# Attention scores on quarter tiles of TensorE, in one pipeline over all batches

## The chip, the cores and the metric

The kernel runs on one core of a Trainium2 chip. The metric is the device time of one launch in microseconds (us); the median of three runs of the kernel before is 711.85 us (710.91 to 712.35). A profile of one further execution shows what each engine did: TensorE (PE; PEld is its loading of weights), VectorE (DVE), ScalarE (ACT), GpSimd (POOL) and SyncE (SP, which issues the transfers).

## What is computed

A causal attention with a window of 64 keys, and an RWKV channel mix on its output. Eight batches, eight heads, 576 positions, head size 64; the model has 512 channels, the mix 1024.

```python
def _attn_ref(q, k, v):                       # (8, 8, 576, 64)
    scores = scale * np.matmul(q, k.transpose(0, 1, 3, 2))
    rel = pos[:, None] - pos[None, :]
    scores = np.where((rel >= 0) & (rel < 64), scores, -1e9)
    ...                                       # softmax over keys
    return np.matmul(attn, v)
def _moe_ref(x, mu_k, mu_r, w_k, w_v, w_r):   # x: (8, 576, 512)
    xk = mu_k * x + (1.0 - mu_k) * x_prev     # x_prev: one position back
    xr = mu_r * x + (1.0 - mu_r) * x_prev
    k = np.maximum(xk @ w_k, 0.0)
    return 1.0 / (1.0 + np.exp(-(xr @ w_r))) * (k * k @ w_v)
```

## The kernel before

**Attention.** A pair of heads fills the 128 partitions: rows 0 to 63 of `q` and `k` belong to one head, 64 to 127 to the other. The 576 queries are nine blocks of 64; a block sees its own keys and those of the block before, 128 in all. One product on the full array makes the scores of a block for both heads (L149). For that the queries stand in `qbd` with zeros where one head's rows meet the other head's columns: `qbd` is 128 rows by (block, head, 64), so the stationary operand is 128x128 of which half is zero. Three blocks are a group (`G`), three groups a pair, and the 32 pairs (8 batches, 4 pairs each) have 288 blocks.

A group runs through these steps, with the tile names that the profile shows:

- `s`, scores on PE (L149, PSUM pool `ps_s`, two buffers), float32; the profile has two instructions for each float32 product.
- `sm` and `nmax` on DVE (L152): mask, scale, minimum; `pr` and `sums` on ACT (L155): the exponential; `rs` on DVE (L158, L159); `pr` times `rs` on POOL (L161).
- `t`, the transposes of the three weights on PE (L168), copied to `pt` by ACT (L170).
- `x`, weights times values on PE (L182): the heads' outputs go to the two halves of the partitions, so each product uses half of the array's columns. Two groups go together (12 products), and ACT copies the result to `xT` (L187).

**Channel mix.** A unit is half a batch, 288 positions; there are 16 units. `time_mix` (L221 to L226) makes `xr` and `xk` on DVE, ACT and POOL. Then come 4 products with `w_r`, 8 with `w_k` and 4 with `w_v`, each 128 outputs wide and accumulated over 12, 12 and 24 instructions (`m`, L235, float32r, PSUM pool `ps_m`, four buffers). ACT, POOL and DVE work on the results (`e`, `th`, `r`; `kf`, `ks`; `r` again), and the output leaves by SP. A unit has 240 instructions of `m`, the kernel 3840.

**Weights.** They come as float64 in 20 chunks of 512 KB (`wst`, L102); five DVE instructions for each chunk (L107 to L113) make float32 of it, ACT and POOL split it in two float32r parts (L116, L117). `w_r` has 4 chunks, `w_k` 8, `w_v` 8, in that order. The first product with `w_v` needs the last chunks.

**Order.** `attention` is a generator of steps for one batch (42 steps); `batches` chains them. At the start 42 steps run, with a chunk of weights at every third from the sixth on; then the first unit's mixing, then `LEAD` = 8 steps more. After that each of a unit's 20 steps takes one or, every 16th time, two attention steps. What the code writes is a priority: a scheduler of the framework orders each engine's instructions, so the order on an engine is not the order of the code.

Of the kernel before, what the change touches and what calls it, by code (L numbers as in the profile page):

```python
# [9 lines left out]
F32 = mybir.dt.float32  # L10
# [3 lines left out]
ALU = mybir.AluOpType  # L14
# [9 lines left out]
NG = NB // G  # L24
# [6 lines left out]
STAGES = 3 * (NP * NG + 2)   # steps of a batch's attention  # L31
# [11 lines left out]
def attn_rwkv_kernel(ctx, tc, qT, kT, v2, mu_k, mu_r, w_k, w_v, w_r, out):  # L43
# [12 lines left out]
    # queries of a pair by block, the heads' apart: zero where a head's rows meet the  # L56
    # other head's columns
    qbd = [const.tile([P, NB, 2, W], F32, name=f"qbd{i}") for i in range(2)]
    nc.vector.memset(qbd[0][:, :G], 0.0)
    nc.vector.memset(qbd[0][:, G:], 0.0)  # L60
# [7 lines left out]
    mask0 = const.tile([P, W], F32, name="mask0")  # L68
    nc.gpsimd.memset(mask, 0.0)
    nc.gpsimd.memset(mask0, 0.0)  # L70
    for h in range(2):
        m = mask[h * W:(h + 1) * W]
        nc.gpsimd.affine_select(out=m, in_=m, compare_op=ALU.is_ge, fill=NEG, base=-1,
                                pattern=[[1, P]], channel_multiplier=-1)
        nc.gpsimd.affine_select(out=m, in_=m, compare_op=ALU.is_ge, fill=NEG, base=W,
                                pattern=[[-1, P]], channel_multiplier=1)
        m = mask0[h * W:(h + 1) * W]
        nc.gpsimd.affine_select(out=m, in_=m, compare_op=ALU.is_ge, fill=NEG, base=0,
                                pattern=[[-1, W]], channel_multiplier=1)

    nc.gpsimd.memset(qbd[1], 0.0)
    # the first group's weights: its first block has none for the other keys
    pr0 = const.tile([P, G, P], F32, name="pr0")
    nc.gpsimd.memset(pr0[:, 0, W:], 0.0)
# [36 lines left out]
    loaded = {}  # L121

    def load_pair(n, cuts=(0, NB)):
        """cuts: the blocks at which q and k are cut into transfers."""
        q = qbd[n % 2]
        k = ld.tile([P, S], F32, name="k")
        for i0, i1 in zip(cuts, cuts[1:]):
            nc.sync.dma_start(k[:, i0 * W:i1 * W], kT[n, :, i0 * W:i1 * W])
            for h in range(2):
                nc.sync.dma_start(q[h * W:(h + 1) * W, i0:i1, h, :],  # L130
                                  qT[n, h * W:(h + 1) * W, i0 * W:i1 * W].rearrange("p (i r) -> p i r", r=W))
        v = ld.tile([P, 2, 4, P], F32, name="v")
        nc.sync.dma_start(v, v2[n])
        loaded[n] = (q, k, v)

    def scores(n, g):
        q, k, _ = loaded[n]
        ps = ps_s.tile([P, G, P], F32, name="s")
        # sm = -(scaled and masked scores), nmax = their minimum
        sm = at.tile([P, G, P], F32, name="sm", bufs=3)  # L140
        nmax = at.tile([P, G], F32, name="nmax", bufs=4)
        pr = pr0 if g == 0 else at.tile([P, G, P], F32, name="pr")
        sums = at.tile([P, G], F32, name="sums", bufs=4)
        # keys of a block's window: the block before and the own one, if there are two
        nks = [W if g == 0 and j == 0 else P for j in range(G)]
        for j, nk in enumerate(nks):
            i = G * g + j
            k0 = (i + 1) * W - nk
            nc.tensor.matmul(ps[:, j, :nk], q[:, i].rearrange("p h r -> p (h r)"),  # L149
                             k[:, k0:k0 + nk], start=True, stop=True)  # L150
# [216 lines left out]
```

## Time and profile before

| | |
|---|---|
| median of 3 runs | 711.85 us |
| span of the profiled execution | 711.3 us |
| PE busy | 682.2 us (96%), 5856 matmul instructions |
| DVE busy | 415.5 us (58%) |
| ACT busy | 413.9 us (58%) |
| POOL busy | 364.9 us (51%) |
| data moved | 56.61 MB, mean 80 GB/s |

In the page's second part each engine has a line of 40 digits, one for each 17.8 us of the span, with the busy share in tenths. The ends of matmuls are modelled and overlap the next ones; so what an instruction costs PE is read from the starts of the instructions around it and not from its own duration. A timeline row gives start, length, engine, line, operation, `out<-in`, the shape and how many instructions are merged in the row (`x12`).

### The profile page before, as it was taken

Reading aid. Unit: us, or ns where it says so; the run is one execution under the profiler, and the core shown is the slowest. Engines: PE = TensorE matmul, PEld = TensorE weight load, DVE = VectorE, ACT = ScalarE, POOL = GpSimd, SP = SyncE. Lnnn points to the kernel's source line nnn. Section 1 sums busy time; section 2 is a strip of 40 time slices with the busy share of each in tenths; the row PEclk is TensorE's granted clock in tenths of the full one; section 3 lists DMA queues with packets and bytes.
Section 4 is the critical chain, followed back from the end, with each engine's and each line's share of the span. In section 5 each row is a group of like instructions: output and inputs, shape, how many; then the busy total and the mean of one; then the engine's idle time right before and its main releaser. Section 6 shows DMA issues by size and latency. Waiting matters only on the chain.

```text
span 711.3 us, 15989 instructions
## 1 busy us (share of the span) xinstructions
PE 682.2 (96%) x5856; PEld 657.9 (92%) x5856; DVE 415.5 (58%) x1326; ACT 413.9 (58%) x1397; POOL 364.9 (51%) x580
## 2 busy tenths in 40 slices
PE   6878878999999999999999999999999999999998
PEld 5766777799999999999999999999999999999998
DVE  3999999955545455465535455463645556463421
ACT  4768775663626383748566575756756475644351
POOL 4788898754335272554626355453624546252420
PEclk9999898999999999999999999999999999999999
DMA  8885666620000001221222222211323221000000
GB/s 208 237 234 152 189 178 176 166 73 26 10 34 2 34 31 64 65 89 45 85 63 72 68 64 88 73 55 44 95 66 94 67 64 48 18 1 35 26 9 34
DMA packets 59742, 56.61 MB, mean 80 GB/s; under 512 B 40592, under 2 KB 49040, under 8 KB 59664
## 3 DMA queue, kind: packets, MB, share of 16 engines
q1 hardware_dynamic: 59664, 55.59, 26.7%
q8 instruction: 46, 0.75, 0.5%
q14 instruction: 32, 0.26, 0.1%
HBM read 46.14 MB, written 9.44 MB: 78 GB/s over the span
## 4 chain that ended last, share of the span: by engine, by line
PE 80%; DVE 15%; POOL 1%; issue 1%; DMA 1%; SPq 1%; ACT 0%
PE m L235 68%; PE s L149 6%; PE x L182 4%; PE t L168 3%; DVE sm L152 2%; DVE wt L111 2%; DVE wt L107 2%; DVE wt L113 2%; DVE xm L224 1%; DVE wt L109 1%; DVE wt L108 1%; DVE rs L158 1%; POOL pr L161 1%; DMA qbd<-qT 1%; DVE d L221 1%
## 5 line engine op out<-in xcount | busy, mean ns | idle before, releaser
L235 PE MATMUL m<-ks,wv_s 128*128 128x288 f32 x1536 | 226.1, 301 | 1.0 <-ACT wv_s L116 0.9
L235 PE MATMUL m<-xk,wk_s 128*128 128x288 f32 x1536 | 221.2, 299 | 2.0 <-POOL wk_s L117 2.0
L161 POOL TENSOR_SCALAR pr<-pr,rs 128x128 f32<-128x128 f32 (+1 forms) x288 | 129.7, 467 | 173.0 <-DVE rs L159 62.4
L235 PEld LDWEIGHTS m<-ks,wv_s 128*128 128x128 f32 x1536 | 208.7, 190 | 2.5 <-ACT wv_s L116 1.3
L235 PEld LDWEIGHTS m<-xk,wk_s 128*128 128x128 f32 x1536 | 207.0, 189 | 3.6 <-POOL wk_s L117 2.2
L155 ACT ACTIVATE pr<-sm,nmax 128x128 f32<-128x128 f32 (+1 forms) x288 | 111.6, 391 | 68.0 <-DVE nmax L152 67.9
L263 POOL TENSOR_TENSOR kf<-kf 128x288 f32<-128x288 f32 x128 | 93.2, 733 | 81.1 <-ACT kf L262 80.1
L266 DVE TENSOR_TENSOR ks<-kf,ks 128x288 fp32r<-128x288 f32 x128 | 72.6, 571 | 71.5 <-ACT ks L265 71.3
L235 PE MATMUL m<-xr,wr_s 128*128 128x288 f32 x768 | 113.1, 299 | 1.0 <-POOL xr L226 1.0
L235 PEld LDWEIGHTS m<-xr,wr_s 128*128 128x128 f32 x768 | 103.5, 188 | 2.4 <-POOL xr L226 1.9
L149 PE MATMUL s<-k,qbd 128*128 128x128 f32 (+1 forms) x576 | 88.4, 294 | 15.7 <-DVE nmax L152 9.0
L149 PEld LDWEIGHTS s<-k,qbd 128*128 128x128 f32 x576 | 79.0, 205 | 19.0 <-DVE nmax L152 11.2
L226 POOL TENSOR_TENSOR xr<-xm,xr 128x288 fp32r<-128x288 f32 x64 | 56.4, 891 | 71.2 <-ACT xr L225 68.4
L152 DVE CUSTOM_DVE_ANT_0 sm<-s,mask 128x128 f32<-128x128 f32 (+1 forms) x288 | 66.7, 276 | 36.1 <-PE s L149 36.0
L262 ACT ACTIVATE kf<-m 128x288 f32<-128x288 f32 x128 | 52.2, 409 | 36.8 <-PE m L235 29.5
L224 DVE SCALAR_TENSOR_TENSOR xm<-d,muk,xT 128x288 f32<-128x288 f32 x64 | 55.2, 862 | 26.7 <-POOL xr L226 26.6
L265 ACT CAST ks<-kf 128x288 fp32r<-128x288 f32 x128 | 55.1, 431 | 24.9 <-POOL kf L263 24.5
L253 DVE SCALAR_TENSOR_TENSOR r<-th,e 128x288 f32<-128x288 f32 x64 | 34.2, 535 | 50.4 <-ACT th L251 50.1
L247 ACT ACTIVATE e<-m 128x288 f32<-128x288 f32 x64 | 26.2, 410 | 60.9 <-PE m L235 60.7
L168 PE MATMUL t<-ident,pr 128*128 128x128 f32 x288 | 55.4, 284 | 6.2 <-POOL pr L161 3.4
L275 DVE SCALAR_TENSOR_TENSOR r<-m,r 128x288 f32<-128x288 f32 x64 | 28.3, 451 | 56.4 <-PE m L235 56.4
L226 POOL TENSOR_TENSOR xk<-xm,xk 128x288 fp32r<-128x288 f32 x64 | 58.5, 933 | 5.2 <-ACT xk L225 5.2
(44 smaller groups left out, 652.7 us busy)
## 6 DMA issues: line engine op xcount, KB each, us to landing
v<-v SPq DMA_DIRECT2D x32, 512.0 KB, 3.6
outT<-r SPq DMA_DIRECT2D x64, 144.0 KB, 1.7
k<-kT SPq DMA_DIRECT2D x31, 288.0 KB, 3.1
qbd<-qT SPq DMA_DIRECT2D x62, 144.0 KB, 3.6
wst<-w_k SPq DMA_DIRECT2D x8, 512.0 KB, 4.1
wst<-w_v SPq DMA_DIRECT2D x8, 512.0 KB, 3.6
wst<-w_r SPq DMA_DIRECT2D x4, 512.0 KB, 7.6
k<-kT SPq DMA_DIRECT2D x1, 192.0 KB, 2.4
```

What stands on the lines that cost most here:

```text
L149: nc.tensor.matmul(ps[:, j, :nk], q[:, i].rearrange("p h r -> p (h r)"), k[:, k0:k0 + nk], start=True, stop=True)
L152: nc.vector.tensor_tensor_reduce(sm[:, j, :nk], ps[:, j, :nk], mask if nk == P else mask0, scale=-SCALE, scalar=FAR, op0=ALU.add, op1=ALU.min,
L155: nc.scalar.activation(pr[:, j, :nk], sm[:, j, :nk], AF.Exp, bias=nmax[:, j:j + 1], scale=-1.0, accum_out=sums[:, j:j + 1])
L161: nc.gpsimd.tensor_scalar(pr[:, j, :nk], pr[:, j, :nk], rs[:, j:j + 1], 1.0, op0=ALU.mult, op1=ALU.mult)
L168: nc.tensor.transpose(ps[:, j, :], pr[:, j, :], ident)
L224: nc.vector.scalar_tensor_tensor(xm, d, mu[:, c:c + 1], xp, op0=ALU.mult, op1=ALU.add)
L226: nc.gpsimd.tensor_sub(xs[:, 1, c], xm, xs[:, 0, c].bitcast(F32))
L235: nc.tensor.matmul(ps, w[:, a, c, col * P:(col + 1) * P], x(c, e), start=(i == 0), stop=(i == last))
L262: nc.scalar.activation(kf, ps, AF.Relu)
L263: nc.gpsimd.tensor_mul(kf, kf, kf)
L265: nc.scalar.copy(ks[:, 0], kf)
L266: nc.vector.tensor_sub(ks[:, 1], kf, ks[:, 0].bitcast(F32))
```

## The change

- **Scores.** `q` is loaded as it is, without zeros. A product takes the 64 rows of one head and the 64 queries of one block as the stationary operand, and 128 keys: it uses a quarter of the array, the row half by the head and the column half by the block. Four such products cover two blocks of both heads. A round is three tiles of two blocks (`slots`), 12 products; the two heads' scores lie in two PSUM tiles. Score products are 576, not 288. DVE, ACT and POOL have as many instructions for them as before (a tile holds two blocks of one head, not one block of two); the 32 that were 64 keys wide are 128 wide.
- **PSUM.** `ps_s` has four buffers (two before), `ps_m` two (four before).
- **Order.** Two pairs are one item of three rounds. `attention` runs over all batches without a break, in four steps for each round; 32 steps run ahead with a chunk of weights at every second from the fifth on, and afterwards the steps are due at 24 for each 40 steps of the mix. `mix_v` takes one round, 12 products.
- **Buffers.** `q`, `k`, `v` have three buffers; `sm` two and not three, `pr` four, `xm` two.

How the scheduler's order changes PE's work, in the middle of the kernel. Each row is a run of like matmuls (`s` scores, `t` transposes, `x` weights times values, `m` channel mix; the last column is the shape of the moving operand, or of the half that is written, and the number of products). Before, from the products with `w_r` of one unit into those with `w_k`:

```order
L235 MATMUL m<-xr,wr_s 128x288 x12
L168 MATMUL t<-ident,pr 128x128 x3
L235 MATMUL m<-xr,wr_s 128x288 x12
L182 MATMUL x<-pt,v 64x64 x12
L235 MATMUL m<-xr,wr_s 128x288 x12
L149 MATMUL s<-k,qbd_83 128x128 x3
L235 MATMUL m<-xr,wr_s 128x288 x12
L168 MATMUL t<-ident,pr_114 128x128 x3
L235 MATMUL m<-xk,wk_s 128x288 x24
L149 MATMUL s<-k,qbd_83 128x128 x3
```

In that stretch PE leaves the full-width array once, for 12 products `x` in a row. At a like place of the changed kernel:

```order
L144 MATMUL s<-k,q 64x128 x2
L183 MATMUL x<-pt,v 64x64
L144 MATMUL s<-k,q 64x128 x3
L246 MATMUL m<-xk,wk_s 128x288 x12
L144 MATMUL s<-k,q 64x128 x3
L246 MATMUL m<-xk,wk_s 128x288 x12
L170 MATMUL t<-ident,pr 128x128 x3
L183 MATMUL x<-pt,v 64x64 x10
L246 MATMUL m<-xk,wk_s 128x288 x24
L170 MATMUL t<-ident,pr 128x128 x3
L183 MATMUL x<-pt,v 64x64
L144 MATMUL s<-k,q 64x128 x6
```

Here it leaves it four times, and runs of `s` and `x` are cut into pieces of 1 to 10 products. Over the whole kernel PE goes from the full array to a part of it and back 70 times before, and 191 times now; 54 times it now goes directly between `s` and `x`, which use different parts. Of the 191 returns, 151 are to `m` and 40 to `t`.

SP's queue at the start (transfers, in the order of issue). Before:

```order
L128 DMA k<-kT 128x576
L130 DMA qbd_83<-qT 64x9x64 x2
L133 DMA v<-v 128x1024
L102 DMA wst<-w_r 128x1024
L128 DMA k<-kT 128x576
L130 DMA qbd_82<-qT 64x9x64 x2
L102 DMA wst<-w_r 128x1024 x2
```

This stands behind the loads of the first pair and of `mu_k`, `mu_r`: the first weights come behind two pairs. Now, behind the same loads:

```order
L122 DMA k<-kT 128x576
L123 DMA q<-qT 128x576
L125 DMA v<-v 128x1024
L122 DMA k<-kT 128x576
L123 DMA q<-qT 128x576
L125 DMA v<-v 128x1024
L96 DMA wst<-w_r 128x1024 x3
```

The first weights now come behind three pairs, and a pair's queries are one transfer.

The diff, cut to the parts that are spoken of:

```diff
-    ps_s = ctx.enter_context(tc.tile_pool(name="ps_s", bufs=2, space=PSUM))
+    ps_s = ctx.enter_context(tc.tile_pool(name="ps_s", bufs=4, space=PSUM))
...
-    ps_m = ctx.enter_context(tc.tile_pool(name="ps_m", bufs=4, space=PSUM))
+    ps_m = ctx.enter_context(tc.tile_pool(name="ps_m", bufs=2, space=PSUM))
...
     def load_pair(n, cuts=(0, NB)):
-        q = qbd[n % 2]
-        k = ld.tile([P, S], F32, name="k")
+        q = ld.tile([P, S], F32, name="q", bufs=3)
+        k = ld.tile([P, S], F32, name="k", bufs=3)
         for i0, i1 in zip(cuts, cuts[1:]):
             nc.sync.dma_start(k[:, i0 * W:i1 * W], kT[n, :, i0 * W:i1 * W])
-            for h in range(2):
-                nc.sync.dma_start(q[h * W:(h + 1) * W, i0:i1, h, :],
-                                  qT[n, h * W:(h + 1) * W, i0 * W:i1 * W].rearrange("p (i r) -> p i r", r=W))
+            nc.sync.dma_start(q[:, i0 * W:i1 * W], qT[n, :, i0 * W:i1 * W])
...
+    def slots(n, g):
+        if g == 1:
+            return [((n, 6), (n, 7)), ((n, 8), (n + 1, 8)), ((n + 1, 6), (n + 1, 7))]
+        n += g // 2
+        return [((n, i), (n, i + 1)) for i in range(0, 2 * G, 2)]
...
-            nc.tensor.matmul(ps[:, j, :nk], q[:, i].rearrange("p h r -> p (h r)"),
-                             k[:, k0:k0 + nk], start=True, stop=True)
+        for e, halves in enumerate(sl):
+            for j, (n, i) in enumerate(halves):
+                q, k, _ = loaded[n]
+                k0 = max(i - 1, 0) * W
+                for h in range(2):
+                    hr = slice(h * W, (h + 1) * W)
+                    nc.tensor.matmul(ps[h][j * W:(j + 1) * W, e, :], q[hr, i * W:(i + 1) * W],
+                                     k[hr, k0:k0 + P], start=True, stop=True)
+        return [soft(ps[h], sl) for h in range(2)]
...
-    for i in range(STAGES):
+    first = STEPS * (ROUNDS + 2)
+    for i in range(first):
         run(ats, 1)
-        if i >= 5 and i % 3 == 0:
+        if i >= 4 and i % 2 == 0:
             run(wl, 1)
...
-            run(ats, 1)
-            if done % 16 == 0:
-                run(ats, 1)
+            due = (done + LEAD) * ROUNDS * STEPS // MOE_STEPS
+            run(ats, due - ran)
+            ran = due
```

More of the change, by code (lines that the diff above doesn't have):

```diff
@@ L23 @@
 G = 3
-NG = NB // G
+NG = 3
 TH = S // 2
@@ L66, in attn_rwkv_kernel @@
     mask = const.tile([P, P], F32, name="mask")
-    mask0 = const.tile([P, W], F32, name="mask0")
+    mask0 = const.tile([P, P], F32, name="mask0")
     nc.gpsimd.memset(mask, 0.0)
     nc.gpsimd.memset(mask0, 0.0)
-    for h in range(2):
[L72 to L84, printed above, removed]
+    for j in range(2):
+        for t in (mask, mask0):
+            m = t[j * W:(j + 1) * W]
+            if t is mask0 and j == 0:
+                nc.gpsimd.affine_select(out=m, in_=m, compare_op=ALU.is_ge, fill=NEG, base=0,
+                                        pattern=[[-1, P]], channel_multiplier=1)
+                continue
+            nc.gpsimd.affine_select(out=m, in_=m, compare_op=ALU.is_ge, fill=NEG, base=-1,
+                                    pattern=[[1, P]], channel_multiplier=-1)
+            nc.gpsimd.affine_select(out=m, in_=m, compare_op=ALU.is_ge, fill=NEG, base=W,
+                                    pattern=[[-1, P]], channel_multiplier=1)
     muk = const.tile([P, NC], F32, name="muk")
@@ new lines, in scores @@
+    def scores(sl):
+        ps = [ps_s.tile([P, G, P], F32, name="s") for _ in range(2)]
+        for e, halves in enumerate(sl):
[7 more added lines that the diff above has]
+        return [soft(ps[h], sl) for h in range(2)]
@@ L141, in scores, with soft @@
+    def soft(ps, sl):
+        sm = at.tile([P, G, P], F32, name="sm", bufs=2)
         nmax = at.tile([P, G], F32, name="nmax", bufs=4)
-        pr = pr0 if g == 0 else at.tile([P, G, P], F32, name="pr")
+        pr = at.tile([P, G, P], F32, name="pr", bufs=4)
         sums = at.tile([P, G], F32, name="sums", bufs=4)
[L145 to L149, printed above, removed]
-                             k[:, k0:k0 + nk], start=True, stop=True)
@@ L166, in flip @@
         ps = ps_t.tile([P, G, P], F32, name="t")
-        for j in range(G):
-            nc.tensor.transpose(ps[:, j, :], pr[:, j, :], ident)
+        for e in range(G):
+            nc.tensor.transpose(ps[:, e, :], pr[:, e, :], ident)
         pt = at.tile([P, G, P], F32, name="pt", bufs=3)
```

106 lines of the change are left out of this document (53 added, 53 removed).

## Prediction

> **What bounds the kernel now.** The page's slices come first, those of PE and of DVE:
>
> ```profile
> PE   6878878999999999999999999999999999999998
> DVE  3999999955545455465535455463645556463421
> ```
>
> In the first eight slices (142 us) DVE is full and PE is not; from there on it is the other way round. DVE's last decode of a weight, in the timeline, marks the border, and a table of the stages (PE, PEld, DVE, ACT, POOL busy; then clock, DMA share, GB/s) shows both sides:
>
> ```profile
> 140.27 0.74 DVE L113 SCALAR_TENSOR_TENSOR wt<-wst,wt 128x512 uint32<-128x512 uint32 x1
> ...
> 0.00:141.00 141.00, 115.78 (x1029) 99.50 (x1029) 125.85 (x470) 95.90 (x361) 112.37 (x173) 0.94 0.68 191
> 141.00:628.50 487.50, 486.78 (x4227) 478.91 (x4227) 258.26 (x804) 287.64 (x953) 227.95 (x377) 1.00 0.19 57
> ```
>
> Up to 141 us DVE decodes and holds the rest: the products with `w_v` need the last chunks. Most of its 15 idle us lie in the first slice. Behind that PE has no gap, and no other engine is busy for 60% of the time. So the time is 141 us, plus what PE has left then, plus a tail; the tail is 3.1 us, since the chain's last piece ends at 708.19 of 711.3:
>
> ```profile
> 628.57 79.62 PE m L235 x600
> ```
>
> **What an instruction costs PE.** Modelled ends overlap, so I take starts. Four stretches of PE's timeline, and one piece of the chain, give everything:
>
> ```profile
> 404.06 1.84 PE L235 MATMUL m<-xr,wr_s 128*128 128x288 f32 x12
> 405.83 0.92 PE L182 MATMUL x<-pt,v 128*64 128x64 f32 x24
> 406.68 1.85 PE L235 MATMUL m<-xr,wr_s 128*128 128x288 f32 x12
> 408.37 0.83 PE L149 MATMUL s<-k,qbd 128*128 128x128 f32 x6
> 408.95 0.52 PE L235 MATMUL m<-xr,wr_s 128*128 128x288 f32 x2
> ```
>
> ```profile
> 244.49 1.84 PE L235 MATMUL m<-xr,wr_s 128*128 128x288 f32 x12
> 246.26 0.57 PE L182 MATMUL x<-pt,v 128*64 128x64 f32 x12
> 246.76 1.85 PE L235 MATMUL m<-xr,wr_s 128*128 128x288 f32 x12
> ...
> 250.28 5.28 PE L235 MATMUL m<-xk,wk_s 128*128 128x288 f32 x38
> 255.39 0.49 PE L168 MATMUL t<-ident,pr 128*128 128x128 f32 x3
> 255.63 0.65 PE L235 MATMUL m<-xk,wk_s 128*128 128x288 f32 x3
> ```
>
> ```profile
> 330.06 3.18 PE m L235 x24
> ```
>
> - `m`: 24 take 3.18 us, 0.1325 each.
> - `s`: from 406.68 to 408.95 are 2.27 us with 12 `m` (1.59) and 6 `s`: 0.68, so 0.113 for one full-width instruction over 128 keys.
> - `t`: from 250.28 to 255.63 are 5.35 us with 38 `m` (5.04): 0.31 for three, 0.105 each.
> - `x`: with 24 instructions from 404.06 to 406.68 are 2.62 us, less 1.59: 1.03. With 12, from 244.49 to 246.76: 2.27 less 1.59, 0.68. So 0.0292 for an instruction, and **0.33 for the visit**: to leave the full array for half of its columns and come back costs as much as 11 such instructions.
>
> PE's groups from 145.94 us on (counts are what matters here) test these prices:
>
> ```profile
> L235 PE MATMUL m<-ks,wv_s 128*128 128x288 f32 x1440 | 207.8, 299 | 0.0
> L235 PE MATMUL m<-xk,wk_s 128*128 128x288 f32 x1440 | 203.7, 298 | 0.0
> L235 PE MATMUL m<-xr,wr_s 128*128 128x288 f32 x720 | 104.6, 299 | 0.0
> L149 PE MATMUL s<-k,qbd 128*128 128x128 f32 (+1 forms) x306 | 42.9, 275 | 0.0
> L168 PE MATMUL t<-ident,pr 128*128 128x128 f32 x174 | 30.7, 272 | 0.0
> L182 PE MATMUL x<-pt,v 128*64 128x64 f32 x708 | 28.0, 226 | 0.0
> ```
>
> With the order's 34 visits: 3600 x 0.1325 + 306 x 0.113 + 174 x 0.105 + 708 x 0.0292 + 34 x 0.33 = 477.0 + 34.6 + 18.3 + 20.7 + 11.2 = 561.8 us. The trace has 708.19 - 145.94 = 562.3. PE there waits for nothing.
>
> **The first stage of the changed kernel.** Ahead of DVE's last decode stood 123 `sm`, 38 pairs of `rs`, 11 `d`, 19 `xm`, 4 `r` and 8 `ks`; now there stand 72, 22, 7, 12, 4 and 0. Gone are 51 `sm`, 16 pairs, 4 `d`, 7 `xm`, 8 `ks`. An `sm` follows the last after 0.21 us in the timeline, and the groups give the rest:
>
> ```profile
> 141.01 0.28 DVE L152 CUSTOM_DVE_ANT_0 sm<-s,mask 128x128 f32<-128x128 f32 x1
> ...
> 141.22 0.28 DVE L152 CUSTOM_DVE_ANT_0 sm<-s,mask 128x128 f32<-128x128 f32 x1
> ```
>
> ```profile
> L266 DVE TENSOR_TENSOR ks<-kf,ks 128x288 fp32r<-128x288 f32 x128 | 72.6, 571 | 71.5 <-ACT ks L265 71.3
> L224 DVE SCALAR_TENSOR_TENSOR xm<-d,muk,xT 128x288 f32<-128x288 f32 x64 | 55.2, 862 | 26.7 <-POOL xr L226 26.6
> L224 DVE SCALAR_TENSOR_TENSOR xm<-d,mur,xT 128x288 f32<-128x288 f32 x64 | 43.0, 673 | 8.9 <-POOL xk L226 8.6
> L221 DVE TENSOR_TENSOR d<-xT 128x288 f32<-128x288 f32 x64 | 37.4, 591 | 11.4 <-ACT xT L187 10.8
> L158 DVE TENSOR_SCALAR rs<-sums 128x3 f32<-128x3 f32 x96 | 24.0, 250 | 26.9 <-ACT pr L155 26.8
> L159 DVE RECIPROCAL rs<-rs 128x3 f32<-128x3 f32 x96 | 16.2, 169 | 1.5
> ```
>
> 51 x 0.21 + 16 x 0.42 + 4 x 0.59 + 7 x 0.77 + 8 x 0.57 = 10.7 + 6.7 + 2.4 + 5.4 + 4.6 = 30 us less. Against that the first weights stand behind one pair more, 1.06 MB:
>
> ```profile
> GB/s 208 237 234 152 189 178 176 166 73 26 10 34 2 34 31 64 65 89 45 85 63 72 68 64 88 73 55 44 95 66 94 67 64 48 18 1 35 26 9 34
> ...
> v<-v SPq DMA_DIRECT2D x32, 512.0 KB, 3.6
> k<-kT SPq DMA_DIRECT2D x31, 288.0 KB, 3.1
> qbd<-qT SPq DMA_DIRECT2D x62, 144.0 KB, 3.6
> ```
>
> At the 208 GB/s of the first slice that is 5 us; `q` in one piece may take some of it back, so 4 (0 to 5). The masks' 32 wider tiles, the `qbd` zeros and the fewer transfers later lie beside other work: nothing. The stage ends at 141 - 30 + 4 = **115 us** (107 to 120).
>
> This is work moved, not saved: it comes later, where DVE has room, but PE has less behind it. I put PE at 96 `m` by then. DVE's and ACT's orders then have four `r` results and two `kf` behind them, 72 `m`, and two `ps_m` buffers hold 24 more.
>
> **What PE has left there.** By its order from that row on, 3744 `m`, 231 `t`, 936 `x` and 834 `s` instructions, 161 visits and 38 direct changes between `s` and `x`.
>
> - `m` 496.1 and `t` 24.3: old prices.
> - Visits: 161 x 0.33 = 53.1. Before it was 11.2 behind the border; this is the large term. The cover that hid the others was DVE's stage. No row shows a visit to quarter tiles; PE leaves the same full array for it, so I take the same price (0.2 to 0.33 for the about 70 that begin with `s`).
> - Direct changes: no row. Between nothing and a whole visit; half, 0.165, makes 6.3 (0 to 12.5). The Trainium skill (TensorEngine Tiling (Array Packing), Key Properties) says that a change of the tiling mode, though not of the tile, drains TensorE. By that none of the 38 is free; no run here shows one.
> - `x`: 936 x 0.0292 = 27.3. Pieces of odd length leave a half idle: taken run by run from the order, at 2 x 0.0584 for a product alone, 3.9 more. 31.2.
> - `s`: the disputed one. Bounds: 0.113, the full-width row over the same 128 keys, if tiles run one by one, and a quarter of it if four run at once. The nearest row is `x`: 0.0292 for 64 columns is half of 0.113 x 64 / 128, so two tiles do run at once. A table of the first moments of a visit shows how:
>
> ```profile
> 405.82:405.85 0.03, 0.02 (x2) 0.02 (x2) 1.00 0.00 0
> ...
> 405.82:405.94 0.12, 0.11 (x3) 0.11 (x5) 1.00 0.00 0
> ```
>
> A visit (the columns are PE, PEld, clock, DMA share, GB/s): two start together, the third 0.1 us later. A product's two instructions go to the same tile; if the second held up the next product, the first would start alone. I read it as tiles that do not wait for each other, and take 0.0292: 834 x 0.0292 = 24.4, and 9.5 for pieces that don't fill four tiles: 33.9.
>
> Sum: 496.1 + 24.3 + 53.1 + 6.3 + 31.2 + 33.9 = 644.9 us. `ps_m` with two buffers is a new wait: PE's next product but one needs the last result read. Cover is a product of 12 `m`, 1.59 us, against a read of 0.4:
>
> ```profile
> L155 ACT ACTIVATE pr<-sm,nmax 128x128 f32<-128x128 f32 x256 | 100.6, 396 | 34.6 <-DVE nmax L152 34.6
> L262 ACT ACTIVATE kf<-m 128x288 f32<-128x288 f32 x128 | 52.2, 409 | 36.8 <-PE m L235 29.5 <-DVE ks L266 6.5 <-issue 0.2
> ```
>
> Only where three exponentials (1.2 us) stand ahead of the read on ACT is PE, with all that is queued on it, late by a few tenths; once or twice in each of 16 units makes 0 to 10, and I take 4. In all 115 + 644.9 + 4 + 3.1 = **767 us**; by the same account the kernel before has 711.3, 0.5 from the median.
>
> **Rivals.**
>
> - *Two tiles at once.* If matmuls start strictly in order, the second instruction of a product waits for the first, and only its end overlaps the next product: two at a time, 0.0584 each, 48.7 and 10.4 for the pieces, 25 more: **792 us**. For it: two is all that the trace shows. Against it: the two that start together. The Trainium skill (TensorE: Matmul & The Clock Gate, The mechanism) gives it as the rule: matmuls start and end in program order. The two first starts above don't agree with that, as far as the records are true.
> - *No tiles at once in the row halves or at all* (the change does not do what it says): `s` 97.4 us, **831 us**. Against it: `x` has two at once.
> - *Visits are cheap*, the one way to the other side: if leaving for quarter tiles and halves in a mixed order costs nothing, 59.4 us fall away and it is **708 us**, faster through the shorter first stage. It decides from 0.02 us a visit down. Against it: 0.33 in both rows.
>
> **How the numbers follow.** Four at once 0.52, two 0.28, one 0.12, cheap visits 0.04, and 0.04 for a first stage that I misread either way. The time is that of the likeliest, 767; with its bounds (first stage -8 to +5, visits -9, direct changes -6 to +6, waits -4 to +6) it alone would be 745 to 785. Two at once lies within 770 to 810. The range 742 to 812 holds nearly all of both. About 0.2% can be told from no change: faster 0.04, same 0.01, slower 0.95.
>
> **What would show it.** Right: DVE's last decode near 115 us; PE full from there; `s` in runs of 12 products at about 0.7 us beside 0.33 for the visit, against 1.4 if two run at once; a gap of about 0.3 around each piece of `x`. Wrong: PE with idle time behind the border that ACT's reads of `m` end; visits whose price is far from 0.33; or a last decode at 130 us or later.

## The result, and the profile after

| | before | after |
|---|---|---|
| median of four runs, us | 712.1 (710.9 to 712.6) | 765.8 (764.5 to 766.1, and 801.5) |
| ratio | 1 | 1.0754 [1.0738, 1.0769] |
| profiled execution: its time, its span | 711.3 span | 764.5, 762.7 span |
| DVE's last decode ends | 141.0 | 111.7 |
| what PE has behind that | 567 | 648 |

The run of the kernel after at 801.5 us was in a slower state, at a lower granted clock (0.824 against 0.95 to 1.00); without it the median is 765.5 us.

The change made the kernel slower by 53.7 us. The slices of PE, of DVE and of the granted clock in the page of the changed kernel:

```profile
PE   5877889999999999999999999999999999999998
DVE  4998995345463444544345544534446343554522
PEclk9755599999999999999999999999999999999999
```

The picture is the one of before with its border moved ahead: DVE is full for the first six slices instead of eight, and PE from the seventh on. The timeline of DVE gives the border, and the table of the stages both sides (PE, PEld, DVE, ACT, POOL busy, then clock, DMA share and GB/s):

```profile
111.00 0.68 DVE L107 SCALAR_TENSOR_TENSOR wt<-wst,wt 128x512 uint32<-128x512 uint32 x1
```

```profile
0.00:111.70 111.70, 86.67 (x710) 65.92 (x710) 96.67 (x314) 60.94 (x219) 82.87 (x111) 0.71 0.57 196
111.70:759.60 647.90, 645.34 (x5722) 594.77 (x5722) 296.26 (x1010) 354.82 (x1178) 274.55 (x469) 1.00 0.17 53
```

So 29 us were won in the first stage, and 81 lost behind it, where PE is busy for 645.3 of 647.9 us and the granted clock is 1.00, as it was before. The table of waits for PE from 111.7 us on, and the chain's last piece, say that this is not idle time, and that the tail is the old one (759.6 of 762.7):

```profile
PE s L144 <- DVE nmax L155: 2.0, 1, 2.0
PE m L246 <- DVE r L286: 1.3, 4, 0.4
```

```profile
721.19 38.41 PE m L246 x288
```

Where it is lost stands in PE's timeline (start, time, count at the end of the row). Here `s` is a quarter-tile product, which is two instructions:

```profile
149.55 1.85 PE L246 MATMUL m<-xr,wr_s 128*128 128x288 f32 x12
151.32 0.43 PE L144 MATMUL s<-k,q 64*64 64x128 f32 x2
151.68 1.86 PE L246 MATMUL m<-xk,wk_s 128*128 128x288 f32 x12
...
238.47 1.85 PE L246 MATMUL m<-xr,wr_s 128*128 128x288 f32 x12
240.25 0.45 PE L144 MATMUL s<-k,q 64*64 64x128 f32 x8
240.63 1.86 PE L246 MATMUL m<-xk,wk_s 128*128 128x288 f32 x12
...
243.54 1.85 PE L246 MATMUL m<-xk,wk_s 128*128 128x288 f32 x12
245.32 0.34 PE L183 MATMUL x<-pt,v 128*64 128x64 f32 x4
245.58 1.85 PE L246 MATMUL m<-xk,wk_s 128*128 128x288 f32 x12
```

Take starts, less the 1.59 us of 12 `m`. From 238.47 to 240.63 are 2.16: four products of `s` cost 0.57. From 243.54 to 245.58 are 2.04: two products of `x` cost 0.45. From 149.55 to 151.68 are 2.13: one product of `s` alone costs 0.54, nearly as much as four. Counted over the trace behind the last decode, PE leaves the full array 160 times and changes directly between `s` and `x` 36 times; before it left it 34 times.

### The profile page after: what moved, and what is told of

It reads as the page before. It is cut to its first block, busy times and chain, and to the rows that moved or that the text cites. A ratio compares the mean times of both kernels' runs of the same rounds, so it can differ in the third digit from the quotient of the medians.

```text
span 762.7 us, 17032 instructions
## 1 busy us (share of the span) xinstructions
PE 732.0 (96%) x6432; PEld 660.7 (87%) x6432; DVE 393.4 (52%) x1324; ACT 415.8 (55%) x1397; POOL 357.4 (47%) x579
## 2 busy tenths in 40 slices
DMA packets 26578, 56.68 MB, mean 74 GB/s; under 512 B 3200, under 2 KB 11904, under 8 KB 26496
## 4 chain that ended last, share of the span: by engine, by line
PE 80%; DVE 12%; POOL 3%; issue 2%; DMA 1%; ACT 1%; SPq 0%; POOLq 0%
PE m L246 65%; PE x L183 6%; PE s L144 6%; PE t L170 4%; DVE xm L235 2%; DVE sm L155 1%; DVE wt L103 1%; DVE wt L105 1%; POOL pr L164 1%; DVE wt L102 1%; DVE wt L107 1%; DMA wst<-w_r 1%; DVE wt L101 1%; DVE d L232 1%; DVE rs L161 1%
## 5 line engine op out<-in xcount | busy, mean ns | idle before, releaser
L246 PE MATMUL m<-ks,wv_s 128*128 128x288 f32 x1536 | 214.7, 298 | 1.3 <-DVE r L286 1.3
L164 POOL TENSOR_SCALAR pr<-pr,rs 128x128 f32<-128x128 f32 x288 | 130.2, 468 | 139.3 <-DVE rs L162 91.9
L246 PE MATMUL m<-xr,wr_s 128*128 128x288 f32 x768 | 121.7, 309 | 1.7 <-ACT xr L236 1.0
L158 ACT ACTIVATE pr<-sm,nmax 128x128 f32<-128x128 f32 x288 | 112.8, 396 | 16.6 <-DVE nmax L155 16.4
L144 PE MATMUL s<-k,q 64*64 64x128 f32 x1152 | 88.4, 320 | 21.4 <-DVE nmax L155 13.3
L144 PEld LDWEIGHTS s<-k,q 64*64 64x64 f32 x1152 | 55.2, 151 | 40.0 <-DVE nmax L155 16.0
L155 DVE CUSTOM_DVE_ANT_0 sm<-s,mask 128x128 f32<-128x128 f32 x288 | 66.1, 283 | 23.9 <-PE s L144 23.9
L183 PEld LDWEIGHTS x<-pt,v 128*64 128x64 f32 x1152 | 53.3, 150 | 25.3 <-issue 20.8
L183 PE MATMUL x<-pt,v 128*64 128x64 f32 x1152 | 71.7, 246 | 1.7 <-ACT xT L189 1.7
L235 DVE SCALAR_TENSOR_TENSOR xm<-d,mur,xT 128x288 f32<-128x288 f32 x64 | 52.5, 820 | 17.2 <-POOL xr L237 13.9
```

What stands on the lines that cost most here:

```text
L144: nc.tensor.matmul(ps[h][j * W:(j + 1) * W, e, :], q[hr, i * W:(i + 1) * W], k[hr, k0:k0 + P], start=True, stop=True)
L155: nc.vector.tensor_tensor_reduce(sm[:, e], ps[:, e], mask0 if sl[e][0][1] == 0 else mask, scale=-SCALE, scalar=FAR, op0=ALU.add, op1=ALU.m ...
L158: nc.scalar.activation(pr[:, e], sm[:, e], AF.Exp, bias=nmax[:, e:e + 1], scale=-1.0, accum_out=sums[:, e:e + 1])
L164: nc.gpsimd.tensor_scalar(pr[:, e], pr[:, e], rs[:, e:e + 1], 1.0, op0=ALU.mult, op1=ALU.mult)
L183: nc.tensor.matmul(ps[h * W:(h + 1) * W, o, :], v[:, a, c, h * W:(h + 1) * W], pts[h][:, e, j * W:(j + 1) * W], start=True, stop=True)
L235: nc.vector.scalar_tensor_tensor(xm, d, mu[:, c:c + 1], xp, op0=ALU.mult, op1=ALU.add)
```

## The experiments

The theory is that of the prediction: the loss is the price of 160 visits, which come from the order in which the scheduler puts the small pieces, and not from the quarter tiles. The rivals are that the new deal of PSUM's banks (two buffers for `m`) makes PE wait; that quarter-tile products are dear in themselves; and that a visit is cheap. The first four runs hold PE's order, and cut its runs or undo a part of the change; the next four follow from their misses; the last four, and e6, leave the order to the scheduler. The table has them all, with the visits and the direct changes behind the last decode as counted in each trace, the start of the last decode, the time from there to PE's last end, and the median. All but the median are of the one profiled execution; that of e11 took 709.5 us, 3.8 above its median.

| run | visits, direct | last decode | PE behind it | median, us |
|---|---|---|---|---|
| before | 34, 0 | 140.3 | 567.9 | 712.1 |
| after | 160, 36 | 111.0 | 648.6 | 765.8 |
| e1 whole runs, held | 78, 0 | 109.1 | 621.2 | 737.2 |
| e2 and `x` beside `s` | 39, 37 | 115.3 | 610.6 | 732.0 |
| e3 e1 with runs cut | 152, 0 | 117.3 | 636.4 | 758.4 |
| e4 e1 with padded scores, late queries | 39, 0 | 130.3 | 607.2 | 742.8 |
| e5 e1 with 4 `m` buffers | 77, 0 | 112.0 | 609.1 | 724.7 |
| e6 after with 4 `m` buffers | 98, 2 | 133.3 | 585.9 | 726.9 |
| e7 e1 with padded scores | 39, 0 | 129.1 | 607.0 | 742.4 |
| e8 e2 with 4 `m` buffers, held from unit 2 | 36, 33 | 130.0 | 577.3 | 711.5 |
| e9 e2's code, 4 `m` buffers, lead 16, not held | 40, 31 | 130.7 | 568.0 | 703.8 |
| e10 the same, lead 15 | 74, 33 | 129.8 | 583.8 | 718.9 |
| e11 the same, lead 9 | 40, 33 | 130.1 | 574.4 | 705.7 |
| e12 e9 with padded scores | 33, 0 | 137.9 | 568.7 | 711.5 |

### e1: PE's order held, so that runs are whole

```diff
+    def pin(ins):
+        return tc.keep_in_program_order(ins)
-                    nc.tensor.matmul(ps[h][j * W:(j + 1) * W, e, :], ...)
+                    pin(nc.tensor.matmul(ps[h][j * W:(j + 1) * W, e, :], ...))
```

The same stands at the transposes, at `x` and at `m`.

> The changed kernel with one difference: every instruction of TensorE is held in the order of the code, so that the 12 quarter-tile products of a group (s) and its 12 half-tile products (x) each run as one piece. By its order 89 visits to part tiles and 6 direct changes between s and x are left, of 191 and 54; the same instructions, pools and data. Theory (the visits are the loss): behind the last decode 77 visits and no direct change are left, so 496.1 for m, 24.6 for t, 28.1 for x, 24.6 for s and 77 x 0.33 = 25.4, about 599 us after 96 m, 604 after 72; with a first stage of 106 to 112 us that is 708 to 722 us, most likely 714, some 50 below the changed kernel. Rival 1 (two ps_m buffers: the new wait is the loss): the buffers are the same and a fixed order hides a wait worse, so 760 us or more. Rival 2 (quarter-tile products are themselves dear, whatever their order): all 1152 instructions are still there, so 750 us or more.

It took 737.2 us, 1.0367 [1.0349, 1.0384] of before. That is 28.5 below the changed kernel, which neither rival gives, and 15 above the theory's upper end. PE's timeline and its table of waits from 112 us on say why:

```profile
193.74 1.85 PE L250 MATMUL m<-xk,wk_s 128*128 128x288 f32 x12
195.52 0.89 PE L148 MATMUL s<-k,q 64*64 64x128 f32 x24
196.33 3.44 PE L250 MATMUL m<-xk,wk_s 128*128 128x288 f32 x24
...
203.37 1.84 PE L250 MATMUL m<-xk,wk_s 128*128 128x288 f32 x12
205.13 0.92 PE L187 MATMUL x<-pt,v 128*64 128x64 f32 x24
205.98 3.45 PE L250 MATMUL m<-ks,wv_s 128*128 128x288 f32 x24
...
225.96 1.84 PE L250 MATMUL m<-xr,wr_s 128*128 128x288 f32 x12
228.49 1.72 PE L250 MATMUL m<-xr,wr_s 128*128 128x288 f32 x11 [0.69 <-ACT th L264]
```

```profile
PE m L250 <- ACT th L264: 8.3, 12, 0.7
PE m L250 <- ACT kf L277: 2.4, 2, 2.0
```

The whole runs cost what the theory says: 12 products of `s` 2.59 - 1.59 = 1.00 us, 12 of `x` 2.61 - 1.59 = 1.02, visit included. But once in most units 12 `m` take 2.53 us (225.96 to 228.49) instead of 1.59, because a buffer of `m` is still to be read by ACT's second reader. This is the prediction's other term, the two `m` buffers: 1.3 us in the scheduler's order, which put pieces of `t`, `x` and `s` between those products (in its trace from 231.00 to 240.25 us), and 12 x 0.9 = 11 here, with 2.4 at the border 13 of the 17.7 us by which PE's part (621.2) passed its account (603.5).

### e2: x beside s

A group's `x` is moved from the end of a step to its head, ahead of a later group's `s`:

```diff
         for t in range(len(items) + 2):
+            if t - 2 in a2:
+                n, g = items[t - 2]
+                mix_v(slots(n, g), a2.pop(t - 2))
...
             if t < len(items):
                 n, g = items[t]
...
             a1.pop(t - 1, None)
-            if t - 2 in a2:
-                n, g = items[t - 2]
-                mix_v(slots(n, g), a2.pop(t - 2))
```

> The kernel of whole runs, with the x products of a group moved into the step of a later group's s products, so that they stand one behind the other: 49 visits and 46 direct changes instead of 89 and 6; all else the same. Theory: 38 visits fewer behind the last decode at 0.33 (12.5) against 37 direct changes at 0.15 to 0.165 (5.6 to 6.1): 6 to 7 us below the kernel of whole runs; its first stage holds two xm, an r and two ks more on DVE (3 us), so 3 to 7 us below in all, about 709 us, which would be below the kernel before the change. If a direct change costs a whole visit: equal to the kernel of whole runs or 3 us above it. If direct changes were free: 10 to 13 us below.

732.0 us, 5.2 below e1, within the expected 3 to 7. The total alone does not price a direct change, since more than the visits differs: the last decode is 6.2 us later, where 3 were expected, 28 `m` fewer are left behind it, and PE's waits for `m` are others (9.9 us for `ks` and `kf`, where e1 has 10.7 for `th` and `kf`). The price is read from e10 below, where nothing waits.

### e3: the runs cut

```diff
         for e, halves in enumerate(sl):
+            if e == 2:
+                yield
```

and the like in the middle of `x`, with the steps around driving the pieces.

> The kernel of whole runs, with each run of 12 s products cut into 8 and 4, and each run of 12 x products into 6 and 6, with m or t between the pieces: 177 visits instead of 89, direct changes 6 as before, the same instructions; pieces of 4 and 8 products still fill the four tiles. Theory: 88 visits more at 0.33 to 0.35 are 29 to 31 us, 26 to 28 of them behind the last decode, and a first stage about 4 us longer (6 more sm, 6 ks ahead of the last decode): 26 to 34 us above the kernel of whole runs, about 742 us. Rival (a visit costs little, and something else of the scheduler's order made the loss): within 5 us of the kernel of whole runs.

758.4 us, 21.2 above e1: less than the 26 to 34 expected and four times what the rival allows. The pieces themselves are as priced (PE's timeline):

```profile
208.17 0.57 PE L191 MATMUL x<-pt,v 128*64 128x64 f32 x12
208.67 1.86 PE L261 MATMUL m<-xk,wk_s 128*128 128x288 f32 x12
210.46 0.57 PE L191 MATMUL x<-pt,v 128*64 128x64 f32 x12
```

From 208.17 to 210.46 are 2.29, so 0.70 for half a run, 1.40 for both, against 1.02 whole: 0.38 for the visit. Behind the last decode 74 visits more made 15.2 us more, with 68 `m` (9.0 us) and about 2 us of the rest less to do, and with less waiting: 5.4 us for `m` in the table of waits from 112 us on, where e1 has 10.7. Counted back, the visits made about 31 us, 0.42 each; why that is a little more than the rows give was not found. The first stage took 8.2 longer and did the work that is missing behind it. That and the shorter waits are why the whole is under 26.

### e4 and e7: the pipeline without the quarter tiles

```diff
-                for h in range(2):
-                    hr = slice(h * W, (h + 1) * W)
-                    pin(nc.tensor.matmul(ps[h][j * W:(j + 1) * W, e, :], q[hr, i * W:(i + 1) * W],
-                                     k[hr, k0:k0 + P], start=True, stop=True))
+                f = 2 * e + j
+                pin(nc.tensor.matmul(ps[f // G][:, f % G, :], q[:, i].rearrange("p h r -> p (h r)"),
+                                     k[:, k0:k0 + P], start=True, stop=True))
```

With it come the zeros in `qbd`, two transfers of `q` for a pair, and two buffers of `q` and `k` in place of three.

> The kernel of whole runs with the scores as before the change: full-width products with zero-padded queries, one for each block (6 of 128 x 128 for a group in place of 12 quarter-tile products), rows of a tile by head, two transfers of q for a pair, and two buffers of q and k; the pipeline over all batches, the other pools and the order in the code as in the kernel of whole runs. It is the pipeline's part of the change without the quarter tiles'. Theory (quarter tiles gain once their runs are whole): s takes 222 x 0.226 = 50.2 instead of 24.6, and 37 visits to s fall away (12.2 to 13): 12 to 14 us more behind the last decode; with a first stage some 4 to 7 us longer (6 more sm, 7 ks ahead of the last decode, padded transfers) 12 to 20 us above the kernel of whole runs, about 730 us. Rival (quarter tiles lose even in whole runs): below the kernel of whole runs by 5 us or more.

e4 took 742.8 us, and does not answer the question: the next pair but one was loaded ahead of the last scores that use the buffer, so that those of blocks 6 to 8 of every second pair take another pair's queries and keys, and wait for that transfer. Its group of `s` shows the wait (busy, mean ns, idle before and its releaser):

```profile
L153 PE MATMUL s<-k,qbd 128*128 128x128 f32 x576 | 84.5, 304 | 18.6 <-DMA qbd<-qT 11.1
```

e7 loads behind the scores:

> The run with padded scores again, with one thing mended: the next pair's queries are loaded behind the scores that still use the buffer, so that these no longer wait for that transfer. All other things as there: full-width products with zero-padded queries, TensorE in the order of whole runs, two buffers for m. Theory (quarter tiles gain once their runs are whole): behind the last decode, 39 products of x runs and 228 or so s at 0.226: for the same m left, 25.6 us more for s and 12.8 less for 37 visits, so 12 to 14 us more than the kernel of whole runs for the same work; the first stage holds 7 ks, 8 xm, 6 sm and 3 d more on DVE (13 us), but with 140 m or so done by then in place of 76. In all 6 to 16 us above the kernel of whole runs, 743 to 753 us. Rival (quarter tiles lose even in whole runs): below 735 us.

742.4 us, 5.2 above e1, just under the expected 6 to 16 and above the rival's 735. With full-width `s` between the products of `m` the waits of e1 were gone too, so the nearer neighbour is e5, which lacks them too (with the other deal of banks): e7 is 17.8 us above it. But none of that lies behind the border: the last decode is 17.1 us later in e7, and PE has 2.1 us less behind it, with 42 `m` fewer. So neither pair shows by itself what the quarter tiles gain on PE. e12 puts the question again, free of the held order.

### e5 and e6: the deal of PSUM's banks

```diff
-    ps_s = ctx.enter_context(tc.tile_pool(name="ps_s", bufs=4, space=PSUM))
+    ps_s = ctx.enter_context(tc.tile_pool(name="ps_s", bufs=2, space=PSUM))
...
-    ps_m = ctx.enter_context(tc.tile_pool(name="ps_m", bufs=2, space=PSUM))
+    ps_m = ctx.enter_context(tc.tile_pool(name="ps_m", bufs=4, space=PSUM))
```

e5 has it on top of e1, where PE's order does not change by it:

> The kernel of whole runs with the banks of PSUM dealt as before the change: two buffers for s and four for m in place of four and two. TensorE's order is held, and is the same instruction for instruction. The kernel of whole runs took 621.2 us behind its last decode, where its instructions and visits add up to about 603.5; each of 12 units shows TensorE idle for 0.69 us ahead of the first products of r, ended by ACT's second read of m. Theory (the visits are the loss, and a fixed order adds waits for the two m buffers that the scheduler's order avoided): those waits go, 10 to 18 us, and the first stage may be up to 3 us longer, so 720 to 728 us. Rival (the 17.7 us are something else, a dearer visit or a clock): 734 to 740 us, as the kernel of whole runs. Rival (the two m buffers, not the visits, are what made the changed kernel slow): below 712 us, the rest of the loss gone.

724.7 us, 12.6 below e1, as the theory said. ACT's second reader is gone from the table of waits; from 120 us on two waits are left in it, of 2.3 and 0.7 us, both for `ks`.

e6 has it alone, in the scheduler's order:

> The changed kernel with the same deal of PSUM's banks as before the change (two buffers for s, four for m) and nothing held: the order is the scheduler's own. It cuts the runs less often: 144 visits and 22 direct changes instead of 191 and 54, of which 98 and 2 stand behind the 228 m that will be done when DVE ends its decodes; and DVE has 99 sm, 31 pairs of rs, 11 d, 18 xm and 8 ks ahead of the last decode instead of 72, 22, 7, 12 and 0. Theory (visits are the loss): a first stage of 111 plus 5.7 + 3.8 + 2.4 + 4.6 + 4.6, about 132 us, and 582 us for what is left, with the tail 717 us (705 to 730): most of the loss comes back with a change of nothing but the deal of the banks, because the order changes with it. Rival (quarter-tile products are dear in themselves): above 750 us. Rival (the waits for two m buffers are the loss, in the scheduler's order too): the same 717 or less, but then the trace of the changed kernel should show TensorE idle behind the border, which it doesn't (1.3 us).

726.9 us, in the range and 10 above its middle: 39 of the 54 lost us come back from two numbers. This does not speak for waits in the changed kernel (its table has 1.3 us for `m`): with the other deal the scheduler makes another order, with 62 visits and 34 direct changes fewer behind the last decode, and more attention ahead of it.

### e8: a first try to beat both

e2's code with e5's deal, and `pin` active only from unit 2 on.

> What the theory says should beat both kernels: the changed kernel with x beside s (as in the second run), two buffers for s and four for m, and TensorE's order held from the third unit on, so that the first stage is left to the scheduler, which has 90 sm, 29 pairs of rs, 11 d, 18 xm and 8 ks of DVE's ahead of the last decode. By its order 72 visits and 46 direct changes, 35 and 33 of them behind 228 m. Theory: first stage 111 + 18.3 = 129 us, then 478.6 for m, 21.7 for t, 24.6 for x, 22.0 for s, 11.6 for visits and 5.1 for direct changes, 563.5 us, tail 3.1: 696 us (688 to 708), below the kernel before. Rival (something besides visits and m buffers still costs, as in the kernel of whole runs): 712 us or more.

711.5 us, ratio 1.0005 [0.9991, 1.0019]: above the theory's 688 to 708, and at the rival's 712. PE waits again where its order is held, once a unit and for another thing, the last `ks` of a unit (table of waits from 140 us on):

```profile
PE m L252 <- DVE ks L283: 3.4, 11, 0.3
```

That is 3.4 of the 15.5 us by which the run passed the 696. Where the rest went is not shown.

### e9, e10, e11: one number

e2's code and e5's deal with nothing held, and `LEAD`, the number of steps by which attention is ahead:

```diff
-LEAD = 8
+LEAD = 16
```

(15 in e10, 9 in e11.)

> The changed kernel with nothing held, two buffers for s and four for m, x beside s, and attention 16 steps ahead of the channel mix in place of 8. The scheduler's own order then has 78 visits and 45 direct changes, 38 and 30 of them behind 228 m, with the same instructions as the changed kernel. Theory: the first stage is as in the run that held the order from the third unit on (130 us), and 562.8 us are left by the old prices; in the two runs before, the kernels took 5 us (scheduler's order) and 14 us (held) more than this account, of which TensorE's idle time behind the last decode, 0 and 8 us, is a part: so 702 us (696 to 709), below both kernels. Rival (what the last runs took above the account is dearer quarter tiles, not waits): 710 us or more.

> The same kernel with the lead at 15 steps in place of 16: a number in the code, and no instruction, buffer or transfer more or less. With it the scheduler cuts the runs up again: 112 visits and 46 direct changes instead of 78 and 45, 72 and 33 of them behind 228 m instead of 38 and 30; the first stage is the same within 1 us. Theory: 34 visits at 0.33 to 0.35, 3 direct changes at 0.15 and 3 to 4 us for pieces that don't fill their tiles: 15 to 17 us above the kernel with lead 16, about 718 us. Rival (visits are cheap in the scheduler's order, where they may lie in gaps): within 4 us of the kernel with lead 16.

> The same kernel with the lead at 9 steps: 77 visits and 47 direct changes, 38 and 33 of them behind 228 m, a first stage of the same length. Theory: within 3 us of the kernel with lead 16, since the runs are as whole, so about 703 us: it is the order and not the lead itself that counts. Rival (the lead itself, more attention done early, is what pays): between the other two or above, 708 us or more.

703.8, 718.9 and 705.7 us: the ratios to before are 0.9903 [0.9877, 0.9929], 1.0103 [1.0086, 1.0120] and 0.9907 [0.9888, 0.9926]. All three are within 3 us of what was expected. e9 beats both kernels, the one before by 1%. e10 does the same work 15.2 us slower. The tables of the stages, of e9 and of e10, show that it is all behind the border, and that PE is full in both:

```profile
0.00:131.40 131.40, 107.89 (x999) 88.05 (x1000) 116.25 (x388) 81.11 (x293) 99.28 (x140) 0.90 0.54 184
131.40:698.80 567.40, 567.36 (x5435) 552.20 (x5434) 290.62 (x938) 335.81 (x1106) 258.33 (x440) 1.00 0.17 57
```

```profile
0.00:130.50 130.50, 107.06 (x988) 86.39 (x990) 116.11 (x387) 80.67 (x290) 101.58 (x141) 0.91 0.56 185
130.50:713.60 583.10, 583.10 (x5450) 559.28 (x5446) 282.00 (x938) 337.50 (x1107) 257.04 (x439) 1.00 0.17 56
```

Why is in PE's timeline of e10, which has a whole pair of runs and a cut one close together:

```profile
221.22 4.22 PE L248 MATMUL m<-xk,wk_s 128*128 128x288 f32 x30
225.37 0.92 PE L185 MATMUL x<-pt,v 128*64 128x64 f32 x24
226.22 0.89 PE L146 MATMUL s<-k,q 64*64 64x128 f32 x24
227.03 3.45 PE L248 MATMUL m<-xk,wk_s 128*128 128x288 f32 x24
...
235.74 2.54 PE L248 MATMUL m<-ks,wv_s 128*128 128x288 f32 x18
238.21 0.80 PE L185 MATMUL x<-pt,v 128*64 128x64 f32 x18
238.93 0.40 PE L248 MATMUL m<-ks,wv_s 128*128 128x288 f32 x1
239.26 0.34 PE L185 MATMUL x<-pt,v 128*64 128x64 f32 x4
239.53 0.67 PE L248 MATMUL m<-ks,wv_s 128*128 128x288 f32 x3
240.13 0.33 PE L185 MATMUL x<-pt,v 128*64 128x64 f32 x2
240.38 0.43 PE L146 MATMUL s<-k,q 64*64 64x128 f32 x2
240.74 0.54 PE L248 MATMUL m<-ks,wv_s 128*128 128x288 f32 x2
241.21 0.88 PE L146 MATMUL s<-k,q 64*64 64x128 f32 x22
242.02 1.85 PE L248 MATMUL m<-ks,wv_s 128*128 128x288 f32 x12
```

The whole pair, from 221.22 to 227.03, is 5.81 less 30 x 0.1325: 1.84 us. The cut pair, from 235.74 to 242.02, is 6.28 less 24 x 0.1325: 3.10 for the same 24 and 24. Three visits more made 1.26 us, 0.42 each, with the pieces that don't fill their tiles in it. And the whole pair is 0.18 less than the two runs apart (1.00 + 1.02, in e1): a visit is saved for a direct change, which so costs 0.15 to 0.17.

### e12: e9 without the quarter tiles

e7's edit on e9.

> The fast kernel (lead 16, two buffers for s and four for m, x beside s, the scheduler's order) with the scores as before the change: full-width products with zero-padded queries, two transfers of q for a pair, two buffers of q and k. Its order has 64 visits, all to x, and no direct change, 33 of them behind 228 m; 120 sm ahead of the last decode instead of 93. So the only thing that it lacks is the quarter tiles. Theory: the account gives 139.3 + 568.0 + 3.1 = 710.4 us against 695.7 for the fast kernel, which took 8 us more than that; with the 5 to 8 us that the scheduler's orders took above their account, 717 us (711 to 724): the quarter tiles gain some 13 us once their runs are whole and each shares its visit with x. Rival (quarter tiles gain nothing at best, and the fast kernel's 1% comes from the rest of the change or from mine): 706 us or less.

711.5 us, 1.0002 [0.9991, 1.0013]: below the expected 711 to 724's middle, above the rival's 706. Both kernels have PE full behind their borders. With e9 at 0.9903, the quarter tiles gain about 1%, 7 to 8 us, where runs are whole and each shares its visit with `x`; that is a bit more than half of the 13 expected. The expectation calls them the only thing that e12 lacks, but `q`'s transfers and zeros and the buffers of `q` and `k` change with them. And PE's part behind the last decode is equal in both (568.0 and 568.7); the gain shows as an earlier border, 130.7 against 137.9, with less of the attention done ahead of it (768 instructions of `s` are left of 1152 in e9, 330 of 576 in e12).

The account met e12 (710.4 against a span of 709.7) and missed e9 by 6 (695.7 against 701.9). Most of that is in the counts: in e9's trace 217 `m` are done at the last decode and not 228, and 40 visits and 31 direct changes follow. With the counts of the trace and the old prices, 3623 `m`, 207 `t`, 840 `x`, 768 `s`, the visits and the direct changes make 567.0 us, where PE took 568.0; the like for e12 is 567.7 of 568.7. For e11 it is 568.5 of 574.4, in an execution that took longer than its median; those 6 us are open.

## Why the prediction was right

**First stage: 115 us forecast, 111.7 measured.** The sum of DVE's work held: DVE was busy for 96.7 us of that stage where it was for 125.9 before, 29.2 less where 30 were forecast. The 4 us for weights that come later were not needed: DVE's first decode starts at 14.61 us, and started at 16.58 before. The first slice moved 319 GB/s where it moved 208, and the transfers have 26578 packets instead of 59742. That `q` in one piece gave back what the further pair's 1.06 MB took fits these numbers; no run tried it alone.

**What is left behind it.** The row was put at 3744 `m`, 231 `t`, 936 `x`, 834 `s`; the trace has 3744, 228, 934 and 816. Visits were put at 161 and direct changes at 38; the trace has 160 and 36. So the count, taken from the order, was as good as a measurement.

The trace's counts also say what the 80.7 us are that PE has more behind the last decode. There are 132 `m`, 48 `t` and 214 `x` more that are no longer done ahead of it, 28.8 us at the old prices; 126 visits more, 42.8 at 0.34; 36 direct changes, 5.8 at 0.16; and the scores take 12.1 less, 816 quarter-tile instructions for 318 full-width ones. That makes 65.3. The other 15 are a little waiting and the pieces that don't fill their tiles, for which the forecast had 13.4. So the quarter tiles did gain 12 us on PE, and the visits, direct changes and pieces that came with the order took about five times as much.

**The price of a visit, 0.33.** No row of before showed a visit to quarter tiles. Now 8 instructions of `s` cost 0.57 and 24 cost 1.00 (e1), so 16 cost 0.43, and what is left at none is 0.35. For `x` it is 1.02 at 24 and 0.45 at 4, so 0.34. The term of 53.1 became about 55.

**Direct changes, 0.165.** 0.15 to 0.17, from e1 and e10. The Trainium skill (TensorEngine Tiling (Array Packing), Key Properties) says that a change of the tiling mode drains TensorE. This agrees with the traces read here, where no such change came free. The page gives no price; half of a visit is what these runs show.

**Four tiles at once, the term with the widest doubt.** Eight products of `s` more cost 0.43 us, 0.054 each. A full-width instruction over the same keys takes 0.113, two of them a product; two tiles at once would make 0.117 a product, four make 0.058. So four. The starts show it as well: a table of the first moments of a run of `s` in e1 (from 195.52 us on), and one of the lone product of `s` at 210.71 us in the changed kernel (columns PE, PEld, clock, DMA share, GB/s):

```profile
195.51:195.54 0.03, 0.02 (x4) 0.02 (x4) 1.00 0.00 0
195.51:195.67 0.16, 0.15 (x4) 0.15 (x8) 1.00 0.96 384
195.51:195.70 0.19, 0.18 (x8) 0.18 (x11) 1.00 0.86 345
```

```profile
210.70:210.86 0.16, 0.15 (x1) 0.16 (x2) 1.00 0.61 231
210.70:210.87 0.17, 0.17 (x2) 0.17 (x2) 1.00 0.60 231
```

In e1 four instructions start within 0.03 us, and the next four about 0.16 us after the first. A lone product's second instruction starts 0.16 us after its first. So the four that start together are the first instructions of four products, and a second instruction does not hold up the next product: the rival of 792 us falls. The rule beside that rival, the Trainium skill's (TensorE: Matmul & The Clock Gate, The mechanism) that matmuls start and end in program order, does not agree with these starts for products on different tiles, if the two instructions of a product stand next to each other in the program, as the prediction took them. The trace does not list the program's order, so that condition is not shown.

**The two `m` buffers, 4 us.** 1.3 us of waits in the table, so the term was small as said. But the four waits there end on DVE's `r`, not on reads that stand behind three exponentials on ACT, as the prediction had it. Held orders (e1) made 11 to 13 us of it, and that is where the expectation of e1 failed: it took over a number that the scheduler's order had made small.

**The sum.** 111.7 + 647.9 + 3.1 = 762.7, and the run lies 1.8 above its span where 0.5 was assumed. The forecast of 767 is 1.2 above the median: the first stage was put 3.3 and the rest 1.0 too high, and the 3.1 us between this span and the median were left out. That these nearly cancel is luck; the terms themselves were right within 4 us. Two slips in the prediction's working change nothing: its bounds add up to 740 to 784 and not 745 to 785, and its prices give the kernel before 710.8 us, where 711.3 is the span of the trace.

**Cheap visits, the rival on the other side**, fell with e3 and e10: same instructions, more visits, 21 and 15 us.

So of the 54 us, the order alone gives back 28.5 (e1), the order and the deal of banks 41 (e5), the deal alone, through the order that it leads to, 39 (e6), and the deal with `x` beside `s`, a lead of 16 and nothing held 62 (e9). That the visits cost what they do is shown. Why the scheduler cuts the runs at a lead of 15 and not of 16 was not tried.

## What to carry to other kernels

Count a smaller tile's gain against the times that TensorE must leave the full array for it: here the visit costs as much as six or seven quarter-tile products, so runs have to be whole, and runs of two tile shapes should stand side by side. When a scheduler makes the order, read the order and count the visits before the chip is used, and try the numbers that move it (leads, buffers): the same work lay between 704 and 766 us. When an order is held by hand, look for the buffers whose waits the scheduler had filled.

## What the runs showed of the hardware that was not expected

- A quarter-tile product alone in a visit costs nearly as much as four: one product of `s` took 0.54 us, four 0.57, twelve 1.00.
- The clock that TensorE was granted was half for longer in the first stage of the changed kernel. Two rows of the table of stretches, from 76 to 95 us, of before and of after (the clock is the third number from the end):

```profile
76.00:95.00 19.00, 16.37 (x141) 14.39 (x140) 18.63 (x71) 13.21 (x49) 16.13 (x24) 0.82 0.58 178
```

```profile
76.00:95.00 19.00, 16.84 (x108) 13.16 (x106) 18.93 (x53) 11.68 (x42) 15.51 (x18) 0.50 0.58 196
```

PE did 108 instructions there in place of 141, in records that fill as much of the time. From 57 to 76 us the clock was 0.50 as well, and 0.91 before. DVE was full in both rows, and from 20 us up to the border its table of waits in the changed kernel names POOL alone (3.9 us), never PE; so nothing shows the clock setting the border. What else it cost was not tried.
